# Forward softmax and PSUM copies in pieces, row copies on GpSimd's DMA queue, products in the array's current shape, and new priorities

## The chip, the cores and the metric

One core of a Trainium2 chip runs the whole program. Its engines are TensorE (PE; its weight loads are listed apart as PEld), VectorE (DVE), ScalarE (ACT), GpSimd (POOL) and SyncE (SP, which only issues DMAs). Each engine works through its own list of instructions in order and waits on semaphores for the others. The metric is the device time of one execution in microseconds, as the median over runs.

## The reference

A sequence of 2,048 tokens of width 512 is normalised. Two branches work on it and their outputs are added to the input: an attention layer with a recurrent memory, and an MLP with a squared ReLU. The kernel computes the output and the gradients of all ten inputs.

```python
x = A_x
xn = _layernorm(x, axis=-1)
return x + _A_ref(xn, A_mem0, A_Wq, A_Wk, A_Wv, A_Wo, A_seg_len) + _B_ref(xn, B_w1, B_b1, B_w2, B_b2)

# _A_ref: 64 segments of 32 tokens, 32 heads of 128, 8 memory rows
for s in range(n_seg):
    h = jnp.concatenate([mem, xs], axis=1)
    q, k, v = (einsum('btd,dhe->bhte', h, W) for W in (Wq, Wk, Wv))
    scores = jnp.where(mask, einsum('bhqe,bhke->bhqk', q, k) * scale, -1e9)
    o = einsum('bhte,hed->btd', einsum('bhqk,bhke->bhqe', softmax(scores), v), Wo)
    mem = o[:, :M, :]                  # the next segment needs it
    outs.append(o[:, M:, :])

# _B_ref: out = relu(x @ w1 + b1)**2 @ w2 + b2
```

Each segment needs the memory rows that the one before produced, so the 64 segments are a chain, forward and, for the gradients, backward.

## The kernel before

The program has five stages. The MLP runs first, forward and most of its backward. The forward scan follows: 64 times `chain(s)`, with the work that depends on no memory row between the links. Then the weights are transposed and the backward scan runs the 64 segments in reverse, again with a `chain(s)`. Last come the weight gradients of the attention (`ps_gw`), dense products over all rows, together with the backward of the normalisation.

A forward link projects q and k of 32 rows (`sg.proj`, ps_q and ps_k, 32 products each in four column strips of the array), copies them out of PSUM (`evict`), transposes them on TensorE (`to_T`, ps_qT and ps_kT), forms the scores onto a mask that a product with the identity has put there (ps_sc, 8 of a row's 40 columns being memory rows of four segments together), and projects v. `weights` takes the maximum over the row (VectorE), subtracts it and applies the exponential (ScalarE, into P40, printed as P). Two VectorE transposes (PTA and PTL, printed as PB) make it ready for the second product (ps_o, in 32\*32 blocks), whose copy out of PSUM also multiplies by the reciprocal of the row sum (oN). A VectorE transpose gives OT, the output projection is ps_RA, and eight small products (ps_mem) put the new memory rows into the next segment's input (PA). GpSimd normalises P for the backward pass (L1020) and adds the MLP's rows (obA, L1194).

Between the links lie: four segments make a block, whose first-eight rows of each segment are handled together in `l_proj` and `l_attn` (names with an L at the end: "late" rows); `dw_unit` computes the gradients of w1 and w2 (ps_dw) from saved activations, two products of 512 columns per row chunk, with the chunk (sx) loaded by SP, 128 rows a load, five buffers; `blk_out` saves the input rows of a block for the weight gradients (hN, S_HNA). In the backward scan `l_pre` and `l_post` do the late rows, and `blk_out` saves the gradient rows (gNat, which is maskL's memory, S_GOA).

None of this is written in the order in which it runs. Each piece is handed to a planner (`_Plan.add`) with a cost per engine, what it reads and what it writes. `_Plan.run` then simulates the engines and picks the next operation by a rank (the longest way to the end, by those costs, plus a number from a table, `BIAS_1` for the forward scan and `BIAS_2` for the backward), and this order is what each engine's list gets. For TensorE every operation has an array shape: "f" whole (128\*128), "w" column strips (128\*32), "d" blocks (32\*32). The planner charges a change of shape. `PAR` holds three numbers per plan: a grace for waits, how long an engine may be left idle for a later operation of higher rank, and a charge against changes of shape.

```python
PAR = ((0.3, 0.3, 0.0), (0.61, 7.94, 4.04), (0.09, 2.05, 17.32))
_TURN = 0.105
```

Of the kernel before, what the change touches and what calls it, by code (L numbers as in the profile page):

```python
# [12 lines left out]
BIAS_1 = {  # L13
    "l_proj": (
        47.2, 6.5, -41.1, 1.2, 0.8, -33.9, -14.2, 11.4, 20.3, -5.1, -5.3, -14.4, 17.4, 1.5, 7, 20.1, 4.7,
        25.3, -22.2, 55.6, -37, 19.3, -97.5, -1.4, 23, -6.1, -29.3, 48.8, 4.1, 4.5, 52.1, -159.3,
    ),
    "blk_in": (
        11.4, -35.6,
    ),  # L20
# [4 lines left out]
    ),  # L25
    "chain": (
# [4 lines left out]
    ),  # L31
    "blk_out": (
        16.8, -102.8, -36.2, -171.6, -10.2, -72.7, -50.6, -74.7, -96.5, 48.6,
    ),
    "l_attn": (
# [53 lines left out]
_LINE = 128  # L89
_FETCH = 4.2  # L90


class _PE(dict):
    shape = None
    n = 8


def pe(cost, shape, n=8):
    x = _PE(PE=cost)
    x.shape = shape  # L100
    x.n = n
    return x
# [1640 lines left out]
```

## Time and profile before

| | |
|---|---|
| Median of 3 runs | 2809.19 us (2799.02 to 2809.37) |
| Profiled execution, first to last instruction | 2798.3 us |
| Mean granted TensorE clock | 0.995 |
| PE busy | 2664.6 us, 54,888 matmul records |
| PEld busy | 1538.5 us |
| DVE busy | 1327.3 us |
| ACT busy | 985.8 us |
| POOL busy | 824.8 us |
| DMA | 530.91 MB, mean 190 GB/s |

Rows of the profile read "line engine operation, output <- input, shape and type, xcount, busy time, mean ns of one, idle time before it and what ended it". A product's shape is given as contracted rows\*output columns of the array, then the columns that stream through. "issue" as a releaser is a wait that the profile cannot lay at another engine's door. The time of a DMA instruction on SP is its issue only; the transfer runs on after it.

### The profile page before, as it was taken

To read this page: it belongs to the slowest core of one execution; us is meant where nothing else is said; L and a number is where in the kernel's file an instruction comes from. 1 tells how busy PE (TensorE), PEld (TensorE's weight loads), DVE (VectorE), ACT (ScalarE), POOL (GpSimd) and SP (SyncE) were. 2 spreads that over 40 slices of the span, in tenths; PEclk is the share of its full clock that TensorE was granted. 3 is DMA by queue.
4 is the path that set the end of the run, shared out by engine and by line. 5 is a ranking of instruction groups with operands and counts; after the bars stand their busy time and mean duration, and the time that the engine had idled before them with its cause. 6 is when DMAs were issued, how large, how long until landed. Compare 5 with 4: busy or idle time off the path is not lost.

```text
span 2798.3 us, 125071 instructions
## 1 busy us (share of the span) xinstructions
PE 2664.6 (95%) x54888; PEld 1538.5 (55%) x55072; DVE 1327.3 (47%) x3327; ACT 985.8 (35%) x2012; POOL 824.8 (29%) x2431
## 2 busy tenths in 40 slices
PE   8998999999999999999999999999999899999999
PEld 6664555555555555575555555555555444444444
DVE  5544455555455555565455455555455402232322
ACT  4333444444444444364444444444444300000000
POOL 1111111111111111145555555555555301112210
PEclk9999999999999999999999999999999999999999
DMA  6657656555557566647777676777766698788861
GB/s 211 202 172 205 180 160 175 164 166 163 156 169 186 169 185 175 177 118 178 187 181 187 179 189 179 189 192 190 188 182 177 201 344 273 232 255 270 257 185 42
DMA packets 499792, 530.91 MB, mean 190 GB/s; under 512 B 223845, under 2 KB 325398, under 8 KB 497070
## 3 DMA queue, kind: packets, MB, share of 16 engines
q1 hardware_dynamic: 480254, 463.06, 59.9%
q0 software_dynamic: 15056, 53.56, 5.6%
q8 instruction: 430, 7.05, 1.1%
q10 hardware_dynamic: 3936, 6.29, 0.7%
q14 instruction: 116, 0.95, 0.1%
HBM read 249.77 MB, written 237.52 MB: 174 GB/s over the span
## 4 chain that ended last, share of the span: by engine, by line
PE 45%; DVE 4%; issue 3%; DMA 3%; ACT 1%; POOL 1%; SPq 0%; DVEq 0%; ACTq 0%; POOLq 0%
PE ps_gw L1690 14%; PE ps_dRA L1370 8%; PE ps_gw L1694 5%; PE ps_gO L538 3%; PE ps_dRL L1370 3%; PE ps_d L624 2%; DMA dLN<-S_GNL 2%; PE ps_d L573 1%; PE ps_d L599 1%; PE ps_gOT L429 1%; PE ps_d L588 1%; PE ps_gm L1524 1%; PE ps_gL L538 1%; PE ps_dL L1481 1%; PE ps_dP L1468 1%
## 5 line engine op out<-in xcount | busy, mean ns | idle before, releaser
L1370 PE MATMUL ps_dRA<-WA,dT 128*32 128x512 bf16 x6144 | 377.0, 381 | 5.3 <-issue 2.5
L1690 PE MATMUL ps_gw<-WA,WB 128*128 128x512 bf16 x1505 | 330.6, 379 | 1.6
L1690 PEld LDWEIGHTS <-WB 128*128 128x128 bf16 x1896 | 185.4, 98 | 225.0 <-issue 1.7
L538 PEld LDWEIGHTS <-PA 128*32 128x32 bf16 x8192 | 195.4, 96 | 192.3 <-DVE PA L1190 22.3
L435 ACT CAST dN<-ps_d 128x512 bf16<-128x512 f32 x372 | 207.4, 590 | 184.7 <-PE ps_d L599 112.3
L1370 PEld LDWEIGHTS <-dT 128*32 128x32 bf16 x6144 | 151.8, 96 | 154.2 <-DVE dT L517 17.3
L433 DVE CAST gwo<-ps_gw 128x512 bf16<-128x512 f32 x64 | 40.0, 685 | 399.9 <-PE ps_gw L1690 268.5
L435 ACT CAST gwo<-ps_gw 128x512 bf16<-128x512 f32 x64 | 33.1, 598 | 510.2 <-PE ps_gw L1690 357.3
L517 DVE STREAM_TRANSPOSE dT<-dN 128x256 f32<-128x256 f32 x384 | 165.4, 437 | 72.1 <-ACT dN L435 66.5
L1020 POOL TENSOR_TENSOR P<-P,rsA 128x320 bf16<-128x320 bf16 x64 | 46.2, 722 | 458.8 <-DVE rsA L1015 244.1
L624 PEld LDWEIGHTS <-PB 32*32 32x32 bf16 x8192 | 119.8, 92 | 76.4 <-DVE PB L1168 23.9
L1701 POOL DMA_DIRECT2D out_dram<-gwo x96 | 71.6, 753 | 293.9 <-ACT gwo L435 265.1
L538 PE MATMUL ps_q<-WA,PA 128*32 128x512 bf16 x2048 | 145.2, 382 | 5.5 <-DVE PA L1190 3.7
L1039 PE MATMUL ps_RA<-WB,OT 128*32 128x256 bf16 x4096 | 129.0, 277 | 17.7 <-DVE OT L517 13.6
L538 PE MATMUL ps_k<-WA,PA 128*32 128x512 bf16 x2048 | 144.9, 381 | 0.3 <-DVE PA L1190 0.3
L435 ACT CAST kN<-ps_k 128x512 bf16<-128x512 f32 x125 | 73.4, 587 | 194.1 <-PE ps_k L538 172.2
L538 PE MATMUL ps_v<-WA,PA 128*32 128x512 bf16 x2048 | 140.7, 379 | 0.0
L1039 PEld LDWEIGHTS <-OT 128*32 128x32 bf16 x4096 | 103.9, 98 | 46.2 <-DVE OT L517 32.0
L538 PE MATMUL ps_gO<-WB,PA 128*32 128x512 bf16 x2048 | 126.4, 380 | 1.0 <-DVE PA L1528 1.0
L611 POOL COPY BDL<-bPLL 32x64 bf16<-32x64 bf16 x256 | 60.4, 236 | 218.4 <-PE ps_d L573 210.4
L433 DVE CAST qN<-ps_q 128x512 bf16<-128x512 f32 x62 | 42.9, 692 | 171.5 <-PE ps_q L538 169.5
L1254 PE MATMUL ps_dw<-sx,anT 128*128 128x512 bf16 x339 | 108.2, 384 | 6.6 <-DMA sx<-S_XN 2.8
(315 smaller groups left out, 5300.8 us busy)
## 6 DMA issues: line engine op xcount, KB each, us to landing
S_GN<-dN SPq DMA_DIRECT2D x192, 256.0 KB
WA<-S_GN SPq DMA_DIRECT2D x150, 256.0 KB
S_Q<-qN SPq DMA_DIRECT2D x64, 256.0 KB
S_K<-kN SPq DMA_DIRECT2D x64, 256.0 KB
S_V<-vN SPq DMA_DIRECT2D x64, 256.0 KB
S_ON<-oN SPq DMA_DIRECT2D x64, 256.0 KB
bqN<-S_Q SPq DMA_DIRECT2D x64, 256.0 KB
bkN<-S_K SPq DMA_DIRECT2D x64, 256.0 KB
```

What stands on the lines that cost most here:

```text
L433: nc.vector.tensor_copy(out, in_)
L435: nc.scalar.copy(out, in_)
L517: self.plan.add({"DVE": 0.445}, lambda e, half=half: nc.vector.transpose(words(dst, half).rearrange("p (i c r) -> p i c r", i=4, c=2), src ...
L538: nc.tensor.matmul(bk()[32 * j:32 * (j + 1), :], lhsT=win(dc), rhs=Wt(dc, c0), start=(dc == 0), stop=(dc == DC - 1), tile_position=(0, 32 ...
L611: f(q_(dst, j)[:, :, j, 0:c], q_(src_f(), j))
L624: nc.tensor.matmul(bk()[32 * j:32 * j + m, k * P:(k + 1) * P], lhsT=lf(j, i), rhs=rf(j, i), start=(k == 0 and x == 0), stop=(x == n - 1), ...
L1039: nc.tensor.matmul(bk()[32 * c:32 * (c + 1), :], lhsT=sg.rows(OTt, i, j), rhs=Wo[:, JQ * i + j, dh * DH:(dh + 1) * DH], start=(i == 0 and ...
L1254: nc.tensor.matmul(bks[x]()[:], lhsT=anT[x][:, c, :], rhs=sx[z][:], start=(c == 0), stop=(c == TC - 1))
L1370: nc.tensor.matmul(bk()[32 * j:32 * (j + 1), :], lhsT=sg.rows(XT, i, j), rhs=wtf(t, i, j), start=(first and i == 0), stop=(last and i == N ...
L1690: nc.tensor.matmul(bks[n](), lhsT=HNc[:, rc, dc * P:(dc + 1) * P], rhs=gns[y][:, hf * 512:(hf + 1) * 512], start=(y == 0), stop=(y == NRC ...
L1694: nc.tensor.matmul(bks[n](), lhsT=gns[y][:, k * P:(k + 1) * P], rhs=GOc[:, rc, :], start=(y == 0), stop=(y == NRC - 1))
L1701: nc.gpsimd.dma_start(outWs[t][dc * P:(dc + 1) * P, 4 * hf:4 * hf + 4, j, :], wt[:].rearrange("p (i e) -> p i e", i=4))
```

## The change

- Forward softmax: the scores of a segment go to two PSUM banks, four of the eight head groups each. Maximum, subtraction, exponential, the copy of the memory columns and both transposes are done once per half. P40 has two buffers. The mask is laid with two sets of products, over the 32 own columns alone.
- Copies out of PSUM: q and k, and their transposes, are copied in two pieces per bank (`evict2`), and the product with the row sums' reciprocal (`by`) also in two. `parts` tells the planner that a key has pieces.
- Array shape: an operation may have more than one shape ("wf"), and then runs in the array's current shape if it can. The products for w1 and w2 (ps_dw) and the transposes of late rows (`to_T` with a prio, wT) have "wf"; in "w" they are issued as four products of 32 columns of the array each.
- DMAs: sx is loaded in pairs of chunks on GpSimd's queue into three buffers; S_VM and S_KM, S_HNL and S_GOL move to that queue. hN and gNat are saved for the memory rows alone (32 columns per 128 by one product set, one DMA a block), and the tokens' rows are copied from S_XN and from grad_out, DRAM to DRAM, on GpSimd's queue (`copy_tokens`). The detours through S_BL and S_OL go.
- The late rows' scores and dP take both column sets in one product each, so half as many.
- `PAR`, `BIAS_1`, `BIAS_2` and some costs are new.

```diff
-PAR = ((0.3, 0.3, 0.0), (0.61, 7.94, 4.04), (0.09, 2.05, 17.32))
+PAR = ((0.3, 0.3, 0.0), (0.0, 0.45, 38.57), (0.09, 138.45, 24.39))
 BIAS_1 = {
...
-                turn = o.shape not in (None, shape)
+                turn = bool(o.shape) and shape not in o.shape
...
+    def transpose_to(ps_ap, in_ap, base=0, form="f"):
+        if form == "w":
+            for c in range(4):
+                x = slice(32 * c, 32 * c + 32)
+                nc.tensor.transpose(ps_ap[x], in_ap[:, x], ident[:], tile_position=(0, 32 * c))
+            return
...
+    def mem_first(t, b):
+        return t[b * P:b * P + RL, :].rearrange("x (c z) -> c x z", c=DC)
+
+    def copy_tokens(b, dst, src):
+        sg.dma(lambda: dst[b * P + RL:(b + 1) * P].rearrange("(r v) d -> r v d", v=SPB),
+               lambda: src[b * P:(b + 1) * P].rearrange("(v r) d -> r v d", r=SEG)[M:], [("tk", b * SPB - 2)], [], cost=0.7, eng="POOL")
...
+        def evict2(self, out_f, bk, in_f, key, prio, cost, n=2):
+            self.plan.parts[key] = [(key, x) for x in range(n)]
+            for x in range(n):
+                c = slice(512 // n * x, 512 // n * (x + 1))
+                self.plan.add(cost, lambda e, c=c: ev({"DVE": "v", "ACT": "s"}[e], out_f(c), in_f(c)), [bk], [(key, x)], prio)
...
-    self.plan.add({"DVE": 0.69, "ACT": 1.18}, sc, [bk, by[0]], [(dst[0], half)], prio)
+    for y in range(2):
...
+        self.plan.add({"DVE": 0.41, "ACT": 0.73}, sc, [bk, by[0]], [(key, y)], prio)
...
-        sg = Stage(plan, pc, {"c": (5, F8), "f": (2, F8), "m": (2, F8), "t": (1, F8)})
+        sg = Stage(plan, pc, {"c": (6, F8), "f": (2, F8), "m": (2, F8), "t": (1, F8)})
...
-                    for c in range(2):
-                        for j in range(JQ):
-                            nc.tensor.matmul(q_(ps, j)[:, i, 32 * c:32 * c + 32], lhsT=qLT[p][:, i, j, :],
-                                             rhs=KT[p][:, :, i * JQ + j, M * c:M * c + M],
+                    for j in range(JQ):
+                        nc.tensor.matmul(q_(ps, j)[:, i, :].rearrange("p (c v k) -> p v c k", c=2, k=M), lhsT=qLT[p][:, i, j, :],
+                                         rhs=KT[p][:, :, i * JQ + j, 0:2 * M].rearrange("p v (c k) -> p v c k", c=2),
...
-            weights(bs_, P40)
-            A({"DVE": 0.18}, lambda e: V.tensor_copy(PLp[v][:, :, M * v:M * (v + 1)], P40[:, :, 0:M]),
...
+            weights(bss, P40, pk)
+            for h in range(2):
+                x = slice(4 * h, 4 * h + 4)
+                A({"DVE": 0.3}, lambda e, x=x: V.transpose(PTA[:, x], P40[:, x, M:KA]), [(pk, h)], [("PTA", h)], 0)
...
-                       [(nm, s)], [(nm + "M", b, v)])
+                       [(nm, s)], [(nm + "M", b, v)], cost=0.7, eng="POOL")
...
-        sx = [tl("sx%d" % x, [P, D]) for x in range(5)]
+        sx = [tl("sx%d" % x, [P, 2, D]) for x in range(3)]
...
-                A(pe(0.435, "f", 2), mm, [("sx", z), ("anT", 0, c // HC), ("anT", 1, c // HC)], [bks[0], bks[1]])
+                A(pe(0.435, "wf", 2), mm, [("sx", z), ("anT", 0, c // HC), ("anT", 1, c // HC)], [bks[0], bks[1]])
```

The built order of TensorE, in the same segment in the middle of the forward scan, where the last products for v end. anT holds the transposed activations, sx the row chunk, and a product's first number is its output columns in the array. Before:

```order
L538 LDWEIGHTS PA
L538 MATMUL ps_v<-WA,PA 32x512
L1254 LDWEIGHTS anT_2676
L1254 MATMUL ps_dw<-sx_2678,anT_2676 128x512
L1254 LDWEIGHTS anT_2677
L1254 MATMUL ps_dw<-sx_2678,anT_2677 128x512
L429 LDWEIGHTS PA
L429 MATMUL ps_hN<-ident,PA 128x128
```

After:

```order
L562 LDWEIGHTS PA
L562 MATMUL ps_v<-WA,PA 32x512
L1309 LDWEIGHTS anT_2676
L1309 MATMUL ps_dw<-sx_2679,anT_2676 32x512
L1309 LDWEIGHTS anT_2676
L1309 MATMUL ps_dw<-sx_2679,anT_2676 32x512
```

The products for w1 and w2 stand at the same place, now as strips like the ones before them.

VectorE, the softmax of one forward segment, from the q copy or the first maximum to the copy of oN. Before:

```order
L433 CAST qN<-ps_q 128x512
L433 COPY qT<-ps_qT 128x512
L433 COPY KT_2646<-ps_kT 128x16x32 x2
L1007 TENSOR_REDUCE mxA<-ps_sc 128x8
L1008 TENSOR_TENSOR stA<-ps_sc,mxA 128x320
L433 CAST vN<-ps_v 128x512
L1166 COPY PLp_2637<-P_2661 128x8x8
L1168 STREAM_TRANSPOSE PB<-P_2661 128x256
L1169 STREAM_TRANSPOSE PB<-PLp_2637 128x256
L1014 TENSOR_REDUCE smA<-P_2661 128x8
L1015 RECIPROCAL rsA<-smA 128x8
L634 TENSOR_TENSOR oN<-ps_o,rsA 128x512
```

After:

```order
L1055 TENSOR_REDUCE mxA<-ps_sc 128x4
L1056 TENSOR_TENSOR stA<-ps_sc,mxA 128x160
L1055 TENSOR_REDUCE mxA<-ps_sc 128x4
L1056 TENSOR_TENSOR stA<-ps_sc,mxA 128x160
L1218 COPY PLp_2635<-P_2659 128x4x8
L1217 STREAM_TRANSPOSE PB<-P_2659 128x128
L1220 STREAM_TRANSPOSE PB<-PLp_2635 128x128
L1063 TENSOR_REDUCE smA<-P_2659 128x8
L1218 COPY PLp_2635<-P_2659 128x4x8
L1217 STREAM_TRANSPOSE PB<-P_2659 128x128
L1064 RECIPROCAL rsA<-smA 128x8
L1220 STREAM_TRANSPOSE PB<-PLp_2635 128x128
```

The first half's transposes stand ahead of the row sums and of the second half's.

GpSimd, about one forward segment, with P the softmax to be normalised and obA the MLP's rows. Before:

```order
L1020 TENSOR_TENSOR P_2661<-P_2661,rsA 128x320
L1021 COPY PLp_2633<-P_2661 128x8x8
L1194 TENSOR_TENSOR obA<-obA,PB 64x256
L479 DMA out_dram<-wt 128x4x128 x2
L1020 TENSOR_TENSOR P_2661<-P_2661,rsA 128x320
```

After:

```order
L1069 TENSOR_TENSOR P_2659<-P_2659,rsA 128x320
L1070 COPY PLp_2635<-P_2659 128x8x8
L497 DMA sx_2680<-S_XN 128x2x512
L497 DMA sx_2678<-S_XN 128x2x512
L497 DMA S_VM<-S_V 4x8192
L497 DMA sx_2679<-S_XN 128x2x512
L1246 TENSOR_TENSOR obA<-obA,PB 64x256
L1273 COPY hM<-PA 128x128
L497 DMA S_KM<-S_K 4x8192
L497 DMA sx_2680<-S_XN 128x2x512
L1069 TENSOR_TENSOR P_2660<-P_2660,rsA 128x320
```

Between two normalisations stand four loads of sx, the copies of S_V's and S_K's memory rows and the copy for hN.

More of the change, by code (lines that the diff above doesn't have):

```diff
@@ L100, in pe @@
     x.shape = shape
-    x.n = n
+    x.n = {k: n * (4 if k == "w" and len(shape) > 1 else 1) for k in shape}
     return x
@@ L577, in blocks, with mixed @@
                            bk, lambda bk=bk: bk()[:], [(dst[0], half)], prio, EV_F)
-        def mixed(self, nm, pre, terms, rkeys, dst, prio, lift=0.0):
-            bks = [self.bank("d", [P, 512], F32, "ps_" + nm) for _ in range(2)]
-            for half in range(2):
+        def mixed(self, nm, pre, terms, rkeys, dst, prio, lift=0.0, full=False, inter=False, kind=None):
+            bks = [self.bank(kind or "d", [P, 512], F32, "ps_" + nm) for _ in range(2)]
+            for half in ((0, 1) if not inter else ()):
                 bk = bks[half]
@@ L592, in mixed, with mm0 @@
                 bk = bks[half]
+                if inter:
+                    def mm0(e, half=half, bk=bk):
+                        for k in range(4):
+                            for x, (lf, rf) in enumerate(pre):
+                                nc.tensor.matmul(bk()[:, k * P:(k + 1) * P], lhsT=lf(4 * half + k), rhs=rf(4 * half + k),
+                                                 start=(k == 0 and x == 0), stop=False, skip_group_check=True)
+                    self.plan.add(pe(0.22 * len(pre), "f", 4 * len(pre)), mm0, rkeys[0](half), [bk], prio, lift=lift)
                 def mm(e, half=half, bk=bk):
@@ L699 @@
+        for i in range(NI):
+            nc.vector.tensor_copy(maskA[:, i, M:KA], mk[:])
         RB = 2 * P
@@ L1280 @@
                 sg.dma(lambda b=b, dst=dst, o=o: dst[(b // BPC) * P:(b // BPC + 1) * P].rearrange(o, b=BPC, k=M)[b % BPC],
-                       lambda b=b, src=src: seg_rows(src, SEG, 0, M)[b * SPB:(b + 1) * SPB], [("tk", b * SPB - 2)], [])
+                       lambda b=b, src=src: seg_rows(src, SEG, 0, M)[b * SPB:(b + 1) * SPB], [("tk", b * SPB - 2)], [], cost=0.7, eng="POOL")
+            copy_tokens(b, S_HNA, S_XN)
+            copy_tokens(b, S_GOA, gflat)
             for v in range(SPB):
```

317 lines of the change are left out of this document (173 added, 144 removed), and 51 rows, old and new, of tables (BIAS_1, BIAS_2).

## The prediction

> **What bounds the kernel now.** I read the granted clock first (0.995 over the span: no throttled run), then the busy time by stage, then the chain that ended last, then the TensorE waits of the forward stage, then one segment row by row. The windows below are the MLP, the forward scan (64 segments), the backward scan (64 segments) and the weight gradients.
>
> ```profile
> core 0: us, PE busy (x) PEld busy (x) DVE busy (x) ACT busy (x) POOL busy (x), PEclk, DMA share, GB/s
> 0.00:228.50 228.50, 214.99 (x1527) 145.51 (x1551) 118.69 (x488) 86.49 (x209) 36.36 (x84) 1.00 0.60 190
> 228.50:1201.50 973.00, 911.43 (x23391) 543.56 (x23500) 514.89 (x1263) 427.22 (x885) 138.19 (x255) 0.99 0.62 173
> ...
> 1235.50:2210.00 974.50, 936.71 (x26438) 560.81 (x26440) 510.75 (x1265) 409.26 (x807) 538.70 (x1912) 1.00 0.71 182
> ...
> 2257.60:2798.30 540.70, 534.65 (x2439) 243.34 (x2487) 146.73 (x240) 33.15 (x64) 93.26 (x136) 1.00 0.74 228
> ...
> PE 45%; DVE 4%; issue 3%; DMA 3%; ACT 1%; POOL 1%; SPq 0%; DVEq 0%; ACTq 0%; POOLq 0%
> ```
>
> TensorE is busy 94% of the forward scan, 96% of the backward scan and 99% of the weight gradients, and it leads the chain. The change leaves the first and last of these stages as they are (769 us), so its gain or loss falls in some 2,000 us: 15.2 us a segment in either scan. Inside the scans a busy TensorE is not a full one. These are TensorE's rows in half of one forward segment (start, length, shape, columns, count):
>
> ```profile
> 693.21 0.60 PE L538 MATMUL ps_k<-WA,PA 128*32 128x512 bf16 x8
> 693.64 0.31 PE L1153 MATMUL ps_sc<-maskA,ident 128*32 128x320 bf16 x4
> 693.89 0.40 PE L429 MATMUL ps_qT<-ident,qN 128*128 128x128 bf16 x4
> 694.12 0.39 PE L429 MATMUL ps_kT<-ident,kN 128*128 128x128 bf16 x4
> 694.34 0.39 PE L429 MATMUL ps_qT<-ident,qN 128*128 128x128 bf16 x4
> 694.57 0.40 PE L429 MATMUL ps_kT<-ident,kN 128*128 128x128 bf16 x4
> 694.89 0.61 PE L538 MATMUL ps_v<-WA,PA 128*32 128x512 bf16 x8
> 695.34 0.27 PE L1161 MATMUL ps_sc<-KT,qT 128*32 128x40 bf16 x16
> 695.44 0.60 PE L538 MATMUL ps_v<-WA,PA 128*32 128x512 bf16 x8
> 695.87 0.27 PE L1161 MATMUL ps_sc<-KT,qT 128*32 128x40 bf16 x16
> ...
> 698.56 0.23 PE L624 MATMUL ps_o<-vN,PB 32*32 32x128 bf16 x4
> ```
>
> The array has three shapes: whole (128\*128), column strips (128\*32), blocks (32\*32). Four transposes take 0.22 to 0.23 us from start to start (694.12 to 694.34); the four before a change of shape take 0.32 (694.57 to 694.89). A change of shape costs 0.10 us. Eight products of 512 columns in strips step by 0.43 (695.44 to 695.87), 0.054 each: four strips run side by side.
>
> **Part 1, fewer changes of shape.** Counted row by row through the built orders, from the first ps_qL to the first ps_gL the array changes shape 550 times before and 364 after, and from there to the last ps_dRL 607 and 485. The w1/w2 gradient products (ps_dw) now run in strips beside the projections, eight for two, at the 0.43 us that eight of ps_v take; a pair of whole ones has the same number of columns. So -186 and -122 at 0.10: -18.6 and -12.2, -31 in all. A change that stood where TensorE waited anyway gives nothing; so the ends are 0 and -31. The stages are 94 and 96% busy, and I take three quarters: **-23**.
>
> **Part 2, forward softmax and copies in pieces.** TensorE's own waits in the forward scan, and those of its weight loads, which run ahead and so wait longer:
>
> ```profile
> PE ps_RA L1039 <- DVE OT L517: 12.7, 15, 2.0
> PE ps_o L624 <- DVE PB L1168: 10.2, 11, 4.1
> PE ps_mem L1185 <- DVE PB L1047: 7.4, 10, 1.1
> PE ps_q L538 <- DVE PA L1190: 3.7, 12, 0.3
> PE ps_o L624 <- issue: 3.4, 5, 1.1
> PE ps_RA L1039 <- issue: 3.0, 5, 0.8
> ...
> PEld L1185 <- DVE PB L1047: 31.0, 59, 1.5
> PEld L1039 <- DVE OT L517: 30.9, 46, 2.2
> PEld L624 <- DVE PB L1168: 23.9, 36, 4.6
> ```
>
> The first two end in rows that pieces can bring forward; the next two hang on the output projection and the memory copy, which stay whole. VectorE in the same segment, and the sizes that price a piece:
>
> ```profile
> 696.23 0.49 DVE L1007 TENSOR_REDUCE mxA<-ps_sc 128x8 f32<-128x320 f32 x1 [0.80 <-PE ps_sc L1161]
> 696.75 0.49 DVE L1008 TENSOR_TENSOR stA<-ps_sc,mxA 128x320 f32<-128x320 f32 x1
> ...
> 698.28 0.40 DVE L1169 STREAM_TRANSPOSE PB<-PLp 128x256 bf16<-128x256 bf16 x1
> 698.61 0.45 DVE L1014 TENSOR_REDUCE smA<-P 128x8 f32<-128x320 bf16 x1
> ...
> L433 DVE CAST qN<-ps_q 128x512 bf16<-128x512 f32 x62 | 42.9, 692 | 171.5 <-PE ps_q L538 169.5 <-DMA S_HNA<-hN 2.0
> L433 DVE COPY R_A<-ps_dRA 128x256 f32<-128x256 f32 x64 | 27.2, 424 | 171.8 <-ACT R_A L435 163.0 <-DMA S_GN<-dN 8.7
> ```
>
> 692 against 424 ns for half the columns: 1.05 ns an element, 0.16 us fixed. A half piece of the 0.49 maximum is then 0.32, of the 0.40 transpose 0.28. Today the maximum starts 0.36 after the last scores are issued (695.87 to 696.23), and ps_o 2.69 after. In pieces the first half's maximum starts 0.36 after 695.34, at 695.70; two maxima and two subtractions end near 697.0, copy and two transposes of that half near 697.7: the first half of ps_o can start some 0.8 us sooner. The second half has the row sums (0.45) and its own pieces in front, until 698.8, so the block ends only 0.3 sooner; its copy out in four pieces on two engines gives another 0.4, the qN and kN pieces 0.2 to 0.3 (0.69 against 0.42). About 0.9 us a segment off the chain of waits. TensorE gains only where it waited: the waits of 12.7 and 10.2, 23 us, are one end, none the other (VectorE gets more to do, below). The order puts filling products elsewhere now and less of it ahead of ps_o, so new short waits appear; half: **-12**.
>
> **Part 3, products saved.** The four mask products of 320 columns (0.25 us, 693.64 to 693.89, less the change of shape 0.15) become eight of 128 (0.11 at 0.054 for 512 columns): 64 x 0.04, some 2 us. Four whole transposes for hN and gN (0.22) become four strip products (0.06) in each of 32 blocks: 5. The late rows' scores and dP have half as many products of twice the columns; I put that at 0.1 a block, 3. Together -10 at one end, 0 at the other if TensorE waits there anyway; three quarters: **-8**. The strip transposes (ps_qLT, ps_kLT, ps_gLT, ps_wT: 1,552 in place of some 390) take the same time if four run side by side, as the identity products of L1153 do (0.15 for four of 320 columns once the change is off).
>
> **Part 4, more instructions.** TensorE's order grows from 106,363 to 109,759 rows. Its code comes by DMA in 16 KB packets, and in the backward scan, at 27.1 products per us against 24.0 forward, it waits for issue more:
>
> ```profile
> q8 instruction: 430, 7.05, 1.1%
> ...
> PE ps_dP L1468 <- issue: 6.2, 9, 0.9
> PE ps_dL L1481 <- issue: 5.3, 4, 2.5
> ```
>
> Forward goes to about 27 per us too (7.7% more products in less time). The backward scan's two rows are 11.5, the forward's two 6.4: 5.1 more. From 0 (its rate stays below) to twice that, +10, since stretches of strip transposes are the densest; I take **+5**. The Trainium skill ("Runtime: NRT & Kernel Launch", section "Instruction fetch mechanics") calls the cost of crossing a 16 KiB boundary mostly hidden; by it this term is 0 and the sum 5 us lower, though the waits above disagree in the densest stretches.
>
> **Part 5, DMAs.** SP loses 494 issues: the sx loads (224 become 112 pairs on GpSimd's queue), S_VM/S_KM (128), the copies through S_BL and S_OL, the hN and gNat rows. GpSimd is busy 138 of 973 us and gets some 300 more issues at 0.5 to 0.8, about 200 us: room enough, and what waits behind them on that engine (the normalised P, obA) feeds only DMAs. In the tail four S_GOA issues stand ahead of the last dLN load, now one: 3 x 0.38 (the sx issue below), -1. At the start sixteen S_BL issues, 6 us of SP's time, go from the first segments; I take 2 of them. Ends 0 and -7: **-3**. VectorE gets about 110 us (64 segments: 0.7 in the softmax, 128 kN pieces of 0.42) and goes from 53 to about 65% of its stage; hidden as long as no piece stands before one that the chain needs.
>
> **Sum.** -23 - 12 - 8 + 5 - 3 = -41 on a span of 2798.3, so 2757 for the span. The median of the runs, 2809.19, is 10.9 above that span (the page gives no other time of this execution; I take the 10.9 as what lies around it), so 2768. Ends: -31 - 23 - 10 + 0 - 7 = -71, and +10 with no gain.
>
> **Rivals.** (a) *The pairs of sx come late*, and the answer is slower. TensorE runs in order, so a late pair holds the chain. Rows:
>
> ```profile
> L479 SPq DMA_DIRECT2D sx<-S_XN x112: 328/383/1767, 781.8 to 1183.6; - x112
> ...
> L479 POOL DMA_DIRECT2D out_dram<-wt x28: 542/678/807, 319.6 to 1208.1; - x28
> ...
> DMA to landing us min/median/max: 2.7/3.7/5.3
> ...
> PE ps_dw L1254 <- DMA sx<-S_XN: 2.8, 4, 1.0
> ```
>
> Today sx costs 2.8 us. An issue on GpSimd takes 0.3 longer (0.68 against 0.38), stands behind the normalisation of P, and three pair buffers replace five single ones. It decides from 41/112 = 0.37 us a pair; if each came late by one other issue and that excess (0.68 + 0.3, about 1 us), +112: 2880. Against it: GpSimd is idle 86% of the stage, and three buffers let pairs be under way before they are used. The Trainium skill ("SBUF — State Buffer", section "Who interferes with whom") says that a DMA issued from GpSimd is starved of its descriptor port while VectorE copies in a two-port mode: it speaks for this rival, and the 0.542 to 0.807 us spread above is what this trace shows of it. (b) *Transposes in strips don't run side by side*: 1,552 at 0.055 in place of 0.014 (a whole one by 0.22/4, a strip one by 0.054/4), +64: 2832. Only the identity products speak against it. (c) *The change does nothing*: the turns fall where TensorE waits, and VectorE's extra 110 us eat the pieces' gain: -10 to +10, about 2809. (d) *The chain is what binds*: with 0.9 us off it in every segment, 64 x 0.9 = 58 in place of part 2's 12: 2722.
>
> **Chances.** The sum 0.60, (d) 0.14, (c) 0.13, (a) 0.08, (b) 0.05. The predicted time is the sum's, 2768. The range leaves out (a), (b) and some of (d): from 2728, between the sum's low end (2738) and (d), to 2815, near (c)'s worse end of 2819. The three runs lie 0.37% apart, so 0.5%, 14 us, is about the least that can be told from no change: faster 0.77 (sum, d, a little of c), same 0.11 (most of c), slower 0.12 (a and b).
>
> **What will show it.** Part 1: fewer rows where the start-to-start step is 0.10 too long, and ps_dw rows in 128\*32. Part 2: the waits for OT and PB below 12.7 and 10.2, first ps_o under 2.2 us after the last scores. Part 4: issue waits in the forward stage near 12. (a) waits of ps_dw for sx over 10 us; (b) four strip transposes 0.2 apart in place of 0.06. Wrong would be a forward stage not under 960 us, or a backward stage that changes by more than 20.

## The result, and the profile after

The changed kernel takes 2894.89 us (median of 4 runs, 2887.15 to 2908.73) against 2809.28 for the kernel before (4 runs): 1.0317 times as long, 95% interval 1.0281 to 1.0352. The forecast was 2768, with a range of 2728 to 2815. The profiled execution spans 2885.4 us against 2798.3, 87.1 more.

Where these 87.1 us lie is seen first in a view of the stages. The columns are: from and to, length, busy time and number of instructions of TensorE, its weight loads, VectorE, ScalarE and GpSimd, the granted clock, the busy share of the DMA engines, GB/s. The rows are the forward scan, the turn, the backward scan and all that follows, of the kernel before:

```profile
228.50:1203.60 975.10, 913.08 (x23452) 545.16 (x23564) 516.95 (x1267) 428.59 (x886) 139.98 (x259) 0.99 0.62 173
1203.60:1235.50 31.90, 27.02 (x520) 25.68 (x508) 24.43 (x46) 21.23 (x32) 14.97 (x36) 0.95 0.57 138
1235.50:2211.50 976.00, 938.21 (x26466) 561.57 (x26464) 510.75 (x1265) 409.69 (x808) 538.70 (x1912) 1.00 0.71 182
2211.50:2798.30 586.80, 571.35 (x2942) 260.59 (x2986) 156.48 (x265) 39.86 (x78) 94.78 (x141) 1.00 0.75 233
```

and of the changed one:

```profile
229.90:1287.50 1057.60, 940.08 (x25454) 562.28 (x25449) 582.46 (x1952) 467.88 (x1221) 337.41 (x579) 0.98 0.61 161
1287.50:1311.90 24.40, 19.71 (x352) 18.49 (x344) 18.32 (x34) 14.60 (x24) 13.50 (x32) 0.86 0.67 156
1311.90:2301.40 989.50, 927.21 (x26448) 556.54 (x26440) 545.39 (x1313) 394.01 (x774) 548.27 (x1927) 1.00 0.69 178
2301.40:2885.40 584.00, 574.11 (x2955) 260.80 (x2950) 155.64 (x262) 38.83 (x76) 95.17 (x142) 0.99 0.76 233
```

The forward scan is 82.5 us longer, the backward scan 13.5; the turn is 7.5 shorter and the end 2.8 shorter, the MLP 1.4 longer. So the loss is in the forward scan. TensorE's busy share fell there from 94 to 89%: it waits more.

The forward scan has blocks of four segments. Means over 15 blocks (the second to the last; for the fourth segment the first to the last but one), from the first ps_q of one segment to that of the next (us), tell two patterns apart at once:

| segment of the block | first | second | third | fourth |
|---|---|---|---|---|
| before | 15.45 | 14.99 | 14.45 | 15.21 |
| after | 18.15 | 15.02 | 14.88 | 17.36 |
| DMA engines busy, before | 0.71 | 0.64 | 0.52 | 0.56 |
| DMA engines busy, after | 0.68 | 0.33 | 0.50 | 0.81 |

The second and third segments are no shorter, although they now hold less work beside the link; the first and fourth are 2 to 3 us longer. An estimate of TensorE's own work (the forecast's 0.054 us for a strip product of 512 columns, other shapes by their share of the array and their columns) goes from 11.9, 12.9, 11.9 and 11.1 us to 12.2, 11.9, 11.3 and 12.5: some of what the fourth segment gains in length is work that the new order put there. The DMA engines' work, much the same in all (0.62 of 975 us and 0.61 of 1,058), has moved into the fourth segment too. The first block, which most of these means leave out, is 6 us longer (81.8 against 75.8); TensorE waits once for 10.3 us there, for GpSimd's copy at L1110.

How the pieces run is seen in the timeline. Two banks of q in a link of the kernel before, one copied by VectorE, one by ScalarE:

```profile
253.12 0.69 DVE L433 CAST qN<-ps_q 128x512 bf16<-128x512 f32 x1 [3.31 <-PE ps_q L538]
253.15 0.60 ACT L435 CAST kN<-ps_k 128x512 bf16<-128x512 f32 x1
253.63 0.62 ACT L435 CAST qN<-ps_q 128x512 bf16<-128x512 f32 x1
254.11 0.63 ACT L435 CAST kN<-ps_k 128x512 bf16<-128x512 f32 x1
```

and the halves of banks in a link of the changed kernel:

```profile
346.30 0.37 ACT L440 CAST kN<-ps_k 128x256 bf16<-128x256 f32 x1 [2.70 <-PE ps_k L562]
346.71 0.42 DVE L438 CAST kN<-ps_k 128x256 bf16<-128x256 f32 x1 [2.04 <-ACT kN L440]
347.22 0.37 ACT L440 CAST qN<-ps_q 128x256 bf16<-128x256 f32 x1 [0.55 <-PE ps_q L562]
347.63 0.42 DVE L438 CAST qN<-ps_q 128x256 bf16<-128x256 f32 x1 [0.49 <-ACT qN L440]
```

Before, the two copies into qN overlap (253.12 to 253.81 and 253.63 to 254.25): two banks, two engines, one destination tile. After, VectorE starts its half 0.04 us after ScalarE ended the other half of the same bank (346.67, 346.71): 0.83 us for what took 0.60 in one piece. The bracket names the releaser: VectorE waited for ScalarE's kN. The groups of the forward scan say that this is the rule:

```profile
L438 DVE CAST qN<-ps_q 128x256 bf16<-128x256 f32 x128 | 54.4, 425 | 76.4 <-ACT qN L440 76.4
L438 DVE CAST kN<-ps_k 128x256 bf16<-128x256 f32 x128 | 54.2, 424 | 120.7 <-ACT kN L440 106.0 <-PE ps_k L562 8.9 <-DMA out_dram<-obA 2.0
L440 ACT COPY KT<-ps_kT 128x256 bf16<-128x256 bf16 x65 | 24.3, 374 | 41.9 <-DVE KT L438 41.9
```

That a half waits for the other half is a semaphore in the program: the releaser that the profile names is the other engine, so one engine at a time is let into a bank. The Trainium skill ("PSUM — Partial Sum Buffer", section "PSUM bank collisions raise a hardware error") gives the ground: the chip does not order two engines in one bank, an overlap is an error, so software has to keep them apart, by bank (more exactly by bank and 32-partition quadrant; these copies span all 128 partitions) and not by address. The rows agree, two banks running side by side and two halves of one not.

The other pattern, in a fourth segment (kernel after, from 622.8 to 642.9 us; 20.1 us in place of 15). Its stages row, and beside it a second segment of the same block:

```profile
593.10:607.80 14.70, 13.86 (x376) 7.71 (x372) 8.21 (x29) 6.73 (x18) 4.03 (x7) 1.00 0.32 113
622.80:642.90 20.10, 16.73 (x424) 9.46 (x419) 11.28 (x34) 7.54 (x20) 6.02 (x11) 0.92 0.87 155
```

The DMA engines are busy 0.87 of it against 0.32. What SP issued there and just before, and who waited:

```profile
620.04 3.57 SPq L1296 DMA_TRANSPOSE anT<-S_AT  x2
629.45 1.19 SPq L1108 DMA_TRANSPOSE PA<-S_XN  x1
...
632.84 1.68 PE L1309 MATMUL ps_dw<-sx,anT 128*32 128x512 bf16 x18 [2.99 <-issue]
633.46 0.53 POOL L497 DMA_DIRECT2D S_KM<-S_K  x1 [10.36 <-DMA S_K<-kN]
```

Two transposing loads of anT stand next to each other in SP's order, and that of PA follows. TensorE stood 2.99 us for "issue", that is, for nothing that the profile can name; GpSimd waited 10.36 us until the store of kN had landed. That TensorE waited for its instructions is read from the DMA queues: from 620.5 to 633 us a single packet of instructions comes,

```profile
q8 instruction: 1, 0.02, 0.5%
```

where the scan has one every 5.3 us on average; it starts at 630.3, the one before it at 618.6, and TensorE goes on at 632.84. Windows around the stall:

```profile
624.00:629.00 5.00, 4.65 (x140) 2.80 (x136) 3.66 (x13) 2.91 (x9) 0.00 (x0) 1.00 1.05 86
```

```profile
629.40:633.40 4.00, 1.01 (x22) 0.33 (x16) 2.06 (x10) 0.75 (x2) 0.00 (x0) 1.00 1.21 260
633.50:636.90 3.40, 3.40 (x82) 1.87 (x74) 0.62 (x2) 0.86 (x3) 2.22 (x4) 0.51 0.59 187
```

While the DMA engines are full (shares over 1, since a packet is counted where it starts) they move 86 GB/s. And after the stall the granted clock is 0.51 for 3.4 us, so that a stall is paid once and half again. In the kernel before, the loads in the middle of the scan stand so:

```profile
557.26 1.43 SPq L1244 DMA_TRANSPOSE anT<-S_AT  x1
562.50 1.40 SPq L1244 DMA_TRANSPOSE anT<-S_AT  x1
594.85 1.57 SPq L1061 DMA_TRANSPOSE PA<-S_XN  x1
597.10 1.23 SPq L1244 DMA_TRANSPOSE anT<-S_AT  x1
601.98 1.26 SPq L1244 DMA_TRANSPOSE anT<-S_AT  x1
```

Of the 55 steps from one load of anT to the next, one is under 2.5 us before and 16 after (under 4 us: 14 and 25). Before, the 56 loads start in all four segments (15, 19, 4 and 18 of them); after, 26 start in the third, 22 in the fourth and 8 in the first. With PA's loads counted in, the steps under 2.5 us are 7 and 16, those under 4 us 25 and 26: it is the closest pairs that are new.

### The profile page after: what moved, and what is told of

Read it like the earlier page. It is cut to its first block, busy times and chain, and to the rows that moved or that the text cites. A ratio compares the mean times of both kernels' runs of the same rounds, so it can differ in the third digit from the quotient of the medians.

```text
span 2885.4 us, 130031 instructions
## 1 busy us (share of the span) xinstructions
PE 2678.9 (93%) x56770; PEld 1544.6 (54%) x56770; DVE 1420.9 (49%) x4051; ACT 1003.6 (35%) x2308; POOL 1030.8 (36%) x2764
## 4 chain that ended last, share of the span: by engine, by line
PE 39%; issue 7%; DVE 5%; DMA 3%; ACT 1%; POOL 1%; SPq 0%; DVEq 0%; ACTq 0%; POOLq 0%
PE ps_gw L1748 14%; PE ps_gw L1752 5%; PE ps_dRA L1429 5%; PE ps_gO L562 3%; PE ps_d L668 2%; PE ps_dRL L1429 2%; DMA dLN<-S_GNL 2%; PE ps_d L605 1%; PE ps_gOT L434 1%; DVE maskA L1418 1%; DMA S_R<-R_A 1%; DVE R_A L438 1%; PE ps_d L642 1%; PE ps_gL L562 1%; PE ps_d L620 1%
## 5 line engine op out<-in xcount | busy, mean ns | idle before, releaser
L655 POOL COPY BDP<-bP 32x256 bf16<-32x256 bf16 x256 | 101.2, 395 | 180.4 <-PE ps_d L605 166.5
L497 POOL DMA_DIRECT2D S_KM<-S_K x64 | 34.0, 531 | 367.7 <-DMA S_K<-kN 305.1
L1088 PE MATMUL ps_RA<-WB,OT 128*32 128x256 bf16 x4096 | 138.0, 277 | 27.9 <-DVE OT L535 23.8
L562 PE MATMUL ps_q<-WA,PA 128*32 128x512 bf16 x2048 | 138.9, 379 | 3.1 <-issue 3.1
L562 PE MATMUL ps_k<-WA,PA 128*32 128x512 bf16 x2048 | 135.8, 381 | 5.7 <-DVE PA L1242 5.1
L1309 PE MATMUL ps_dw<-sx,anT 128*32 128x512 bf16 (+1 forms) x1750 | 123.7, 383 | 4.8 <-issue 4.3
L438 DVE CAST kN<-ps_k 128x256 bf16<-128x256 f32 x128 | 54.2, 424 | 120.7 <-ACT kN L440 106.0
L438 DVE COPY gOT<-ps_gOT 128x512 bf16<-128x512 bf16 x125 | 52.0, 417 | 119.1 <-PE ps_gOT L434 118.9
```

Source lines behind the costliest of these rows:

```text
L438: nc.vector.tensor_copy(out, in_)
L562: nc.tensor.matmul(bk()[32 * j:32 * (j + 1), :], lhsT=win(dc), rhs=Wt(dc, c0), start=(dc == 0), stop=(dc == DC - 1), tile_position=(0, 32 ...
L655: f(q_(dst, j)[:, :, j, 0:c], q_(src_f(), j))
L1088: nc.tensor.matmul(bk()[32 * c:32 * (c + 1), :], lhsT=sg.rows(OTt, i, j), rhs=Wo[:, JQ * i + j, dh * DH:(dh + 1) * DH], start=(i == 0 and ...
L1309: nc.tensor.matmul(bks[x]()[m:m + w, :], lhsT=anT[x][:, c, m:m + w], rhs=sx[z][:, c % 2, :], start=(c == 0), stop=(c == TC - 1), tile_posi ...
```

## The experiments

Two theories. "In turn": the pieces of a bank run one after the other, and the order was laid out as if they ran together. "Bunched transfers": the new order puts the transposing loads close together, in two segments of a block, and what else goes by DMA, instructions first, comes late. Rivals: GpSimd's queue (rival a of the forecast, in a wider form) and instruction fetch as such. Every kernel that keeps the changed one's own order differs from it in nothing but its edit. Times stand against the kernel before on the same chip.

### One copy per bank

```diff
-                c = slice(512 // n * x, 512 // n * (x + 1))
-                self.plan.add(cost, lambda e, c=c: ev(...), [bk], [(key, x)], prio)
+                c = slice(0, 512)
+                self.plan.add(cost, lambda e, c=c, x=x: ev(...) if x == 0 else None, [bk], [(key, x)], prio)
```

and the same for the product with the row sums' reciprocal (oN).

> The changed kernel in its own order, but each bank of q, k, qT, kT and o is copied out of PSUM by one instruction, on the engine that had the first piece; the second piece is not issued. Theory 'in turn' (two pieces of one bank never run side by side: the second waits for the first, 0.37 + 0.04 + 0.42 us in place of one copy of 0.59 or 0.69, and the order was laid out as if they ran together): the forward scan loses most of its 80 us, 2820 to 2850. Theory 'GpSimd queue' (what stands behind the waits for S_K on GpSimd comes late) and theory 'fetch' (TensorE waits for its instructions): no change, 2880 to 2905.

2869.23 against 2804.28, ratio 1.0244 (1.0212 to 1.0277): 65 us slower than before in place of 86. In the right direction, and a third of what the theory expected. The second and third segments of a block fell to 14.14 and 14.23 (from 15.02 and 14.88), 0.8 us a segment; the first and fourth stayed at 17.87 and 17.74. There something else holds, which the saving ran into. It also lost more to the clock: 68.3 us of the forward scan at half clock, against 37.5.

### GpSimd's queue

```diff
-            q = {"SP": nc.sync, "POOL": nc.gpsimd, "ACT": nc.scalar}[eng]
-            self.plan.add({eng: cost}, ...
+            q = {"SP": nc.sync, "POOL": nc.gpsimd, "ACT": nc.scalar, "POOLSP": nc.sync}[eng]
+            self.plan.add({eng[:4]: cost}, ...
```

> The changed kernel in its own order, but every DMA that the change moved to GpSimd's queue (the sx pairs, S_KM and S_VM, the token copies, S_HNL and S_GOL) is issued by SP at the same place of the order. Theory 'GpSimd queue': 50 to 80 us back, 2815 to 2845, and the waits of wt for its earlier store (22 us on ScalarE) go. Theory 'in turn' and theory 'fetch': 2875 to 2910.

2890.70 against 2804.28, ratio 1.0302 (1.0275 to 1.0328): no gain. So GpSimd's long waits (S_KM for S_K, 305 us in all) are not by themselves the loss. But the waits changed in kind: TensorE's issue waits in the forward scan (summed over waits of 0.3 us and more, here and below) fell from 26.4 to 5.4 us, and its waits for DMAs rose from 7.0 to 28.4, most of them for VM. The edit also drew the loads of anT apart on SP's list (6 steps under 2.5 us in place of 16). What the queue is worth with everything else held still is not shown; that moving the issues back mends the kernel falls.

### Whole-array products again

```diff
-                    w = 32 if e == "w" else P
+                    w = P
```

and no `form=e` at the transposes of late rows and of wt.

> The changed kernel in its own order, but ps_dw and the transposes of late rows and of wt are always whole-array products: TensorE's order has 104,639 rows in place of 109,571 and the array changes shape 648 times in place of 364 (forward) and 541 in place of 485 (backward). Theory 'fetch': the waits for instructions in the forward scan fall by about 20 us, the 340 changes of shape at 0.10 cost 34: 2900 to 2912. Theory 'in turn': only the changes of shape count, and some stand where TensorE waits: 2910 to 2930. If strip products themselves were the loss: under 2880.

2919.77 against 2804.28, ratio 1.0413 (1.0390 to 1.0436): 30 us slower than the changed kernel. In this order the strips are worth 30 us, which is near 340 changes of shape at 0.10. It is no clean price: the two scans stand 34 us more at half clock (61.4 and 13.7 us against 37.5 and 3.4), so up to 17 of the 30 us can be the clock's. TensorE's issue waits in the forward scan are 17.0 us here, 26.4 in the changed kernel and 6.1 in the one before: fewer instructions do shorten that wait, by a third, but the kernel as a whole got slower.

### The strips alone, in the order of before

```diff
+            now = None
             for o, e in seq:
+                if e == "PE" and o.shape:
+                    if getattr(o.cost, "any", 0):
+                        e = now = now if now == "w" else "f"
+                    else:
+                        now = o.shape
                 o.fn(e)
```

with `any` set for ps_dw and those transposes, which then take the shape that the array has.

> The kernel before in its own order, with one part of the change alone: ps_dw and the transposes of late rows and of wt run in column strips where the array stands in strips, else whole. Changes of shape 550 to 372 (forward) and 607 to 555 (backward), 230 at 0.10 = 23 us; TensorE's order grows from 106,175 to 109,547 rows. Part 1 as predicted (three quarters of 0.10 each, and 5 back for more instructions): 2797. If strips cost what the changes of shape save, or more instructions do: 2805 to 2820.

2811.34 against 2804.28, ratio 1.0027 (1.0016 to 1.0039): 230 changes of shape fewer and no gain. The forward scan took 974.3 us (975.1), the backward scan 980.4 (976.0). TensorE waited more instead, in the forward scan 53.3 us in waits of 0.3 us and more (48.1 before), among them ps_dw for sx 9.2 us (2.8), ps_mem for PB 10.7 (7.4).

### Two halves of a bank on two engines, alone

```diff
+            def two(e):
+                for x in range(2):
+                    c = slice(256 * x, 256 * (x + 1))
+                    ev({"DVE": "vs", "ACT": "sv"}[e][x], out_f(c), in_f(c))
+            self.plan.add(cost, two, [bk], W, prio)
```

for the copies of q and k in the kernel before.

> The kernel before in its own order, with one part of the change alone: each PSUM bank of q and k is copied out in two halves, the first on the engine that had the whole, the second on the other (VectorE or ScalarE). Theory 'in turn': the second half starts when the first ends, 0.37 + 0.04 + 0.42 = 0.83 us in place of 0.59 (ScalarE) or 0.69 (VectorE); 0.14 to 0.24 later at the last bank of each of 64 links: 2815 to 2830. If halves ran side by side: 0.2 sooner a link, 2792 to 2798.

2847.74 against 2802.96, ratio 1.0162 (1.0131 to 1.0193): 45 us slower, more than either expectation. The forward scan takes it all (1018.0 against 975.1), and every segment of a block is longer (15.89, 15.85, 15.28, 16.04; by 0.4 us the first, by 0.8 to 0.9 the others). Its groups, where the releasers are now the other engine:

```profile
L433 DVE CAST kN<-ps_k 128x256 bf16<-128x256 f32 x128 | 54.3, 425 | 197.5 <-ACT kN L435 179.5 <-DMA obL<-S_BL 5.8 <-DMA S_VL<-vLN 5.8
L435 ACT CAST qN<-ps_q 128x256 bf16<-128x256 f32 x128 | 47.6, 373 | 58.3 <-DVE qN L433 54.2 <-PE ps_q L538 0.4
```

and the end of the copies in the link shown above:

```profile
253.32 0.39 ACT L435 CAST kN<-ps_k 128x256 bf16<-128x256 f32 x1
253.58 0.41 ACT L435 CAST qN<-ps_q 128x256 bf16<-128x256 f32 x1
253.75 0.42 DVE L433 CAST kN<-ps_k 128x256 bf16<-128x256 f32 x1 [3.77 <-DMA anT<-S_AT]
254.09 0.75 DVE L433 CAST qN<-ps_q 128x256 bf16<-128x256 f32 x2
254.87 0.37 ACT L435 CAST qN<-ps_q 128x256 bf16<-128x256 f32 x1 [0.88 <-DVE qN L433]
255.13 0.38 ACT L435 CAST kN<-ps_k 128x256 bf16<-128x256 f32 x1
255.55 0.42 DVE L433 CAST kN<-ps_k 128x256 bf16<-128x256 f32 x1 [0.71 <-ACT kN L435]
```

The last copy ends at 255.97, 2.31 us after the last product of k; with whole ones it ended at 254.74, 1.24 us after it. Four banks in eight halves, each pair tied across two engines, make one chain: the price of a pair is not only 0.2 us, it is handed on to the next bank. This is "in turn" shown by itself.

### Plain loads in place of transposing ones, after and before

```diff
-                    ... nc.sync.dma_start_transpose(
-                        anT[x][:, HC * y:HC * (y + 1), :], S_[2 * u + x, :, HC * P * y:HC * P * (y + 1)]),
+                    ... nc.sync.dma_start(
+                        anT[x][:, HC * y:HC * (y + 1), :], S_[2 * u + x, :, HC * P * y:HC * P * (y + 1)].rearrange("f (c t) -> f c t", t=P)),
```

> The changed kernel in its own order, with the 56 transposing loads of anT replaced by plain loads of the same bytes to the same place (the gradients of w1 and w2 are then formed from untransposed activations). Theory 'bunched transfers' (the order now puts the loads of anT and PA of a block close together, in the last two segments of a block, where the DMA engines reach 81% of their time and more, and instructions, VM and stores come late): the segments of kinds 3 and 0 lose most of their 2 to 3 us, 2835 to 2860. Theory 'in turn' alone: 2880 to 2900.

> The kernel before in its own order, with the same replacement of the 56 transposing loads of anT by plain ones (again without the transposition). Theory 'bunched transfers': before has them spread over the block, so that little is gained, 2790 to 2806. If the loads cost the same wherever they stand, the gain is that of the changed kernel, 2745 to 2775.

The changed kernel: 2853.90 against 2802.96, ratio 1.0189 (1.0160 to 1.0218), 35 us better than it was. The kernel before: 2788.90, ratio 0.9953 (0.9937 to 0.9970), 14 us better. First and fourth segments of the changed kernel fell to 16.63 and 16.03, the second and third stayed (15.11, 15.18): the mirror of the first experiment. The loads cost 14 us in the order of before, and some 20 more where they are bunched. TensorE's issue waits in the forward scan fall with them, from 26.4 to 4.1 us (one profiled execution each; 6.1 to 5.1 in the kernel before).

A plain load also holds SP for less time (0.38 us; a transposing load of the changed kernel 1.8, median). Whether it is the DMA engines alone that are in the way, or SP's list as well, these runs don't tell apart.

### Both at once

The two edits above together.

> The changed kernel in its own order, with both: one copy per PSUM bank (second piece not issued) and plain loads of anT. If 'in turn' and 'bunched transfers' are separate causes their gains add up: 2810 to 2840. If one hides behind the other, it stays within 10 us of the better of the two alone.

2808.80 against 2802.96, ratio 1.0025 (1.0009 to 1.0041). Of 86 us 80 are gone, though the edits brought 21 and 35 alone: each hid part of the other. Some 14 of the 80 are what plain loads are worth in the kernel before as well: against that kernel with plain loads (2788.90) this one is still 20 us behind. All four positions fell (16.28, 14.17, 14.13, 15.64).

### The loads spread, nothing left out

After the order is made, the loads of anT alone are moved later in it; every engine but SP keeps its list.

```diff
+        for k, (o, e) in enumerate(seq):
+            ...
+            t = begin[k]
+            if getattr(o.fn, "moves", False) and begin[k] > 13:
+                u = min(at[x.idx] for x in o.users)
+                t = max(t, last + 9.0)
+                for f in fixed:
+                    if abs(t - f) < 6.0:
+                        t = f + 9.0
+                t = max(begin[k], min(t, begin[u] - 8.0))
+                ...
+            last = max(last, t)
```

> The changed kernel with its own order on all engines but SP's: of the 56 transposing loads of anT most are issued later, at least 9 us after the one before and away from those of PA, and 8 us before their first use. Nothing is left out. Theory 'bunched transfers': the gain of the plain loads (37 us) less the 14 that plain loads were worth in the kernel before, 2860 to 2875. If these loads cost the same wherever they stand: 2880 to 2895.

> The same later loads of anT, and one copy per PSUM bank (second piece not issued). 'In turn' and 'bunched transfers' together: 14 us above the 2809 of the run with plain loads, 2815 to 2835, with few halved clock windows in the forward scan. If spreading the loads does nothing: as the run with one copy per bank alone, 2860 to 2875.

2863.26 against 2802.11, ratio 1.0218 (1.0201 to 1.0235), and with one copy per bank 2829.48, ratio 1.0100 (1.0080 to 1.0120). Both inside what "bunched transfers" expected. The forward scan of the second:

```profile
229.80:1220.60 990.80, 911.17 (x25447) 557.09 (x25446) 571.53 (x1620) 397.72 (x803) 336.79 (x579) 0.99 0.63 172
```

It moves the same bytes through the same queue as the kernel with one copy per bank, whose forward scan took 1035.3: 44.5 us come from where 56 loads stand. TensorE's issue waits in that scan fell from 33.8 to 16.8 us, and without the one copy per bank from 26.4 to 16.8. The time at half clock fell from 68.3 to 13.7 us, and from 37.5 to 17.1. What is left to the kernel before is 27 us: 16 in this row, 17 in the backward scan, less 7 in the turn.

### The same rule for the kernel before

> The kernel before in its own order on all engines but SP's, with the same rule for the loads of anT as in the spread runs above (9 us after the one before, away from those of PA). Plain loads were worth 14 us there: 2790 to 2800 if their nearness is the cost, 2803 to 2808 if it is the loads themselves.

2805.53 against 2804.55, ratio 1.0005 (0.9989 to 1.0020): nothing. The second half of what was expected: there the 14 us are the loads themselves. The rule took away the 14 steps under 4 us that this order has (the shortest is now 4.5 us) and that was worth nothing, so in this order steps of 2.5 to 4 us between loads of anT cost nothing that shows.

### A version made from this

One copy per bank, softmax in halves, the spread loads, and in the planner

```diff
+                    for w in o.banks:
+                        for d in touched.get(id(w), ()):
+                            if d.eng != e:
+                                t = max(t, after(d, e, g))
```

with the forward scan's priorities searched anew for the planner's own end.

> The changed kernel with what the runs point to: one copy per PSUM bank (the softmax stays in halves, which lie in two banks), a planner that lets no two engines into one bank at a time, priorities for the forward scan (one table, three numbers) searched anew with that planner, and the spread loads of anT. If 'in turn' and 'bunched transfers' were the whole loss and the rest of the change is worth something: 2780 to 2800, faster than both. If what else the change brings (more instructions, the backward scan's 14 us) weighs more: 2805 to 2830.

2874.48 against 2804.55, ratio 1.0247 (1.0225 to 1.0269): outside both ranges. The forward scan took 1010.7 us, 36 more than in the kernel before, and the backward scan 1022.4, 46 more, although only the forward scan's priorities were searched anew; the planner's rule on banks changes the backward order as well. In the forward scan the first and fourth segments took 16.65 and 16.57 us with the DMA engines busy 0.79 and 0.71 of them, and TensorE's issue waits were 30.1 us. In the backward scan the issue waits were 23.9 us (15.7 before) and 37.5 us stood at half clock (3.4 before). The planner knows the banks, but neither the DMA engines nor what they do to instruction packets. None of the versions with the transposition in place beats the kernel before, and why its order is so much kinder to the transfers stays open.

## Why the prediction was wrong, step by step

**The failing step is in Part 2**: "its copy out in four pieces on two engines gives another 0.4, the qN and kN pieces 0.2 to 0.3". The sign is wrong. Pieces of a bank on two engines cost 45 us alone (b_pieces), where Part 2 as a whole had -12 between 0 and -23. In the changed kernel one copy per bank gives back 21 us with the loads as they stand, 34 with them spread and 45 with plain ones. What the row for the size of a piece said was read only for its 424 ns: that R_A group ended most of its idle time with "ACT R_A L435 163.0", half a bank on VectorE waiting for the other half on ScalarE, in the kernel before.

The softmax in halves, whose scores lie in two banks, showed the sign that the forecast named: from the last scores to the first ps_o it now takes 2.07 us (median over 63 links; 2.81 before; under 2.2 was forecast). Yet the 0.8 us of this term was not gained. The scores themselves take longer, and from the first scores to the first ps_RA the table has 6.16 us against 6.20. Steps of a link, means in us:

| step | before | after |
|---|---|---|
| ps_q and ps_k, to the first transpose | 3.80 | 4.11 |
| transposes, to the first scores | 1.46 | 1.85 |
| scores | 0.62 | 0.99 |
| to the first ps_o | 2.86 | 2.54 |
| ps_o | 1.09 | 1.53 |
| to the first ps_RA | 1.63 | 1.10 |
| ps_RA, to ps_mem | 3.16 | 3.77 |
| ps_mem, to the next projection | 0.62 | 0.68 |

Two gains of 0.3 and 0.5 against losses everywhere else, those at the copies of q, k and their transposes (0.7) by the waits shown. What makes the scores, ps_o and ps_RA longer is not shown.

**Missing from the sum: what the new order does to the transfers.** Part 5 counted issues and queues and put -3 on them; moving the issues back to SP indeed gains nothing (a_sp). But the loads of anT, which the change does not touch in number or queue, now stand next to each other, and that cost some 24 us alone (a_spread) and 38 where each bank has one copy (am_spread against a_merge, each by its distance from the kernel before). With one copy per bank and the loads spread 27 of the 86 us stay, 17 of them in the backward scan, and these are not explained. SP's list has two loads side by side (620.04 above); the forecast looked at TensorE's and VectorE's orders and at which queue a transfer is on, not at which transfers run at once.

**Part 1** (-23): nothing was found against the count, and 30 us for 340 changes (a_full) lie near the price, if the clock's part is left aside. But in the order of before 230 changes fewer brought nothing (b_cur), so the price is not paid in every order. "94% busy, three quarters of it counts" was the wrong inference: a busy share does not tell which wait ends last.

**Part 4** (+5, 0 to +10): right in sign and too small for the forward scan, and its cause was only in part the one named. The issue waits went from 6.1 to 26.4 us in the forward scan, where 12 were forecast, and from 15.7 to 6.6 in the backward scan. Whole-array products, with some 5,000 rows fewer in TensorE's order, leave 17.0 (a_full); the same instructions with plain loads leave 4.1 (a_plain). So the number of instructions has a part in it, and what else goes by DMA when they are due a larger one. Of the 26.4 us 18.7 stand in fourth segments and 0.6 in second ones. The Trainium skill's "mostly hidden" for a 16 KiB boundary ("Runtime: NRT & Kernel Launch", "Instruction fetch mechanics") holds in the second segments and not in the fourth; the measured 2.99 us decides.

**Part 3** (-8) can't be seen by itself. The transposes in strips run side by side as assumed (four in 0.056 us from start to start, median), and rival (b) falls.

**The 10.9 us** that the sum adds for what lies around the span are not there: in all runs here the time is 1.7 to 1.9 us above the span. The profiled execution of before was simply a quick one. Without this the forecast would have been some 9 us lower, and further off.

**The rivals.** (a) named 2880, close to what was measured, but by another way: TensorE waited 0.5 us for sx in all, not 1 us a pair, and putting the pairs back on SP gained nothing. That the number lies near is chance and says nothing for its mechanism. The test for (a) in the forecast, waits of ps_dw for sx over 10 us, was the right one, and it failed. The two that made most of the loss, a wait made by the pieces themselves and transfers that now meet, were not among the rivals. The forecast's own sign of being wrong, a forward stage not under 960 us, came: 1057.6.

**The backward scan**, 13.5 us longer, is not settled. Its waits there:

```profile
PE ps_dP L1525 <- DVE gOT L438: 20.0, 18, 2.4
PE ps_d L642 <- DVE maskA L1418: 12.3, 27, 1.1
```

These two were 0.8 and 3.4 before. VectorE's copy comes late; which of the order, the numbers of `PAR` and the late rows' new products makes it so was not tried. One copy per bank and the spread loads do not mend it: with both the backward scan is 17 us longer than before.

## What to carry to other kernels

Before a copy is cut in pieces for two engines, look for a pair of that kind in the trace and read its releaser: two engines share the work of two PSUM banks, not of one, so a bank is cut only when it is also made two. When an order is made anew, list which large transfers, transposing ones above all, now start within a few us of each other, whatever queue they are on: their total can stay the same and each segment that holds them still pay (0.9 to 1.6 us here, by what spreading the loads gave back in first and fourth segments), in late instructions too. And a saving on a busy engine counts only where that engine ends the wait; the cheapest test is the saving alone in the old order.

## What the runs showed of the hardware that was not expected

- A stall of TensorE is paid beyond its length. In the forward scans of the fourteen profiled executions, the granted clock went to half (during the gap or within 3.6 us of its end) after a gap of 3 us or more in 36 of 36 cases, after 2 to 3 us in 24 of 37 and after 1.5 to 2 us in 6 of 32; the time at half clock is 3.41 us or a multiple of it. That was 20.5 us of the scan before, 37.5 after, 68.3 with one copy per bank. The Trainium skill ("TensorE: Matmul & The Clock Gate", section "What's actually happening") has the half rate after at least one idle window of some 3.4 us; here gaps of little over 2 us can be enough (17 of 27 that had no other gap of 1 us near them).
- Transposing loads fill the DMA engines at 86 GB/s (the window from 624 to 629 us above). The Trainium skill ("Advanced Engine Details and Errata", section "X-Bar Transpose (TRN2)") calls them as fast as regular ones; for these (128 rows of 1,024 tokens, two-byte elements) the trace disagrees, and plain loads of the same bytes made both kernels faster (14 and 35 us).
- TensorE's instruction packets come by DMA too (queue q8), and the program's own transfers can delay them: 11.7 us without one and a wait of 2.99 us near 630 us in the changed kernel, and issue waits of 26.4, 16.8 and 4.1 us in the forward scan with the loads of anT bunched, spread and plain.
